# Batch 1's second product as seven block products of two tiles, fourteen of its units in the stretch that makes its input, three half sums of the weights on Pool

## The chip, the cores and the metric

The kernel runs on one core of one Trainium2 chip. The metric is the device time of one execution in microseconds (us); the median of three runs of the kernel before is 203.49 us (203.19 to 203.52). The engines are TensorE (PE), VectorE (DVE), ScalarE (ACT), GpSimd (Pool) and SyncE (SP), each with a queue of its own that it works off in order.

## The reference

For each of 8 batches an attention read between 512 tokens x and 32 state rows (8 heads of 64) gives 512 rows "xread" and 32 rows "sread"; both go through a feed-forward network with weights of 512 x 2048 and 2048 x 512 and a leaky relu between.

```python
scores = scale * x @ state.T          # per batch and head: 512 x 32
a = softmax(scores);   xread = a @ state
scores2 = scale * state @ x.T         # 32 x 512
a2 = softmax(scores2); sread = a2 @ x
x = concat([xread, sread]) as rows of 512 (8 heads x 64): 8 * 544 rows
h = x @ w_in; g = max(0.01 * h, h); out = g @ w_out
```

## The kernel before, in words

**First product, by batch.** xread @ w_in is taken together: M = state @ w_in (`a_m`, evicted by `m_evict`) is small, and `ff1(a, hT, s)` gives block s (of 16) of the hidden layer as M's columns times the softmax `aT` (two matmuls of 512 columns into a PSUM tile of tag ph, which has two buffers), after which ACT's Prelu (L397) writes block s of hT. `ff1_pair` does two blocks into the bank "big", with one Prelu (L407). The 16 steps s = 0 to 15 of a batch are one stretch.

**Second product.** hT @ w_out is done in two ways. `piece(b, hT, i, jq)` (L599) does a quarter of the 16 blocks for one tile i of 128 tokens, with four matmuls of 512 columns. `Batch` does four tiles at once by a seven-product scheme for 2 x 2 block matrices: the blocks are A11, A12, A21, A22 of hT and B11 to B22 of w_out, four sums of each (`Fast.sums` su0 to su3 on DVE, L659; `weights_sum` tw0 to tw3, L636), and products n in the order 1, 2, 6, 5, 7, 3, 4. A unit (n, m) (L670) is one of eight terms of product n: one matmul of 256 columns for each tile row, two with `Batch`, one with `Half`. Two banks of tag py take all seven products in turn: product 1, 6, 7 and 4 one after the other on the first, 2, 5 and 3 on the second. Between them ACT copies the bank out (`save`, L679) and DVE joins it to an earlier copy (`join`, L682).

**Which batch uses what.** Batch 0 uses pieces for all four tiles. Batch 1 uses pieces for tiles 0 and 1 and `Half(h1)` for tiles 2 and 3. Batches 2 to 7 use `Batch`. Of a batch's 56 units, 15 (OWN) are done in its own stretch, the rest in the next one's; `PACE` lists how many units follow each ff1, and `PACE2` does so for batch 2's stretch, where `Half` does its own.

**The softmaxes of the next batch** are worked in the current stretch: `a_scores` (L211), then on DVE `a_shift` (L221, L229, L234), `a_max2` (L283, L285), on ACT `a_exp` (L241) and twice `a_exp2` (L291), on DVE `a_probs` (L246, L250, L253, L258, L259: aT) and `a_probs2` (L297, L299: the reciprocal of the row sums r2). In batch 1's stretch that is a2, and in batch 2's a3.

**Buffers.** The tiles of pool att have two buffers unless they say otherwise; r2, which a_exp2 opens (L290) and a_probs2 reads, has two. A tile that takes over a buffer waits for the last reader of the one before it. The four tw tiles lie in buffers of their own.

**Order.** Nothing is scheduled: the order of each engine's queue is that of the program text. The loop of batch 1's stretch is L1061 to L1083, that of batches 2 to 7 is L1097 to L1229.

Of the kernel before, what the change touches and what calls it, by code (L numbers as in the profile page):

```python
# [9 lines left out]
P = 128  # L10
# [3 lines left out]
DM = 512  # L14
# [16 lines left out]
def kernel(  # L31
# [9 lines left out]
    nc = tc.nc  # L41
# [229 lines left out]
    def a_exp(a):  # L271
        a.e1 = block_exp(a.sh, NB)
# [415 lines left out]
    class Batch:  # L688
        def __init__(self, b, hT):
            saved = {n: (spool, t, 1) for n, t in ((1, "sv1"), (6, "sv6"), (5, "sv1"), (7, "sv7"))}  # L690
            self.b, self.f = b, Fast(hT[:], 2 * P, [(spool, f"su{n}", 1) for n in range(4)], saved)
            self.units = [(n, m) for n in (1, 2, 6, 5, 7, 3, 4) for m in range(NM)]
            own = [(n, m) for n in (1, 2) for m in range(6)] + [(1, 6), (2, 6), (1, 7)]
            assert len(own) == OWN
            self.units = own + [u for u in self.units if u not in own]
            self.bank = {}
            self.yos = {}
# [51 lines left out]
                f.join(self.yo(1)[:, :, :HC], bank, 7)  # L749
                self.out(1)  # L750

    class Half(Batch):


        def __init__(self, hT):
            super().__init__(1, hT)
            self.f.__init__(hT[:, :, 2 * P:], P, self.f.homes, self.f.saved)
            self.units = [(n, m) for n in (1, 2, 6, 5, 7, 3, 4) for m in range(NM)]

        def yo(self, r):  # L760
            if r not in self.yos:
                self.yos[r] = ypool.tile([P, 1, DM], FP32, name="ysb", tag="ysb", bufs=3)
            return self.yos[r]

        def out(self, r, cols=slice(0, DM), i=None, eng=nc.sync):
            eng.dma_start(rows_of(1)[2 + r], self.yo(r)[:, 0, :])

    OWN = 15
    PACE = (1, 4, 4, 4, 3, 4, 4, 3, 4, 4, 4, 4, 3, 4, 3, 3)
    PACE2 = (0,) * 10 + (3, 3, 2, 2, 2, 3)  # L770

    att_of = [Attn() for _ in range(B)]
    a0, a1, a2 = att_of[:3]
# [269 lines left out]
    a_probs(a1)  # L1043
    for i in range(NT):
        piece(0, h0, i, 2)
    for i in (2, 3):
        piece(0, h0, i, 3, copy=None)
    for i in (2, 3):
        y_store(0, i, VEC)
    for h in range(0, H, 2):  # L1050
        cast_x(3, h, h + 2, POO)
    a_a2t(a0)
    weights_sum(2, 4, 8)
    weights_sum(1, 4, 8)
    weights_sum(0)

    h1 = hpool.tile([P, 16, S], BF16, name="hT", tag="hT")
    fill = [(0, h0, 0, 3), (0, h0, 1, 3)] + [(1, h1, i, jq) for jq in range(3) for i in range(2)]  # L1060
    for s in range(16):  # L1061
        if s in (6, 10):
            ff1_pair(a1, h1, s, "big")
        elif s not in (7, 11):
            ff1(a1, h1, s)
        if s % 2:
            pb, hT, i, jq = fill[s // 2]
            piece(pb, hT, i, jq)
        if s == 3:
            a_scores(a2)  # L1070
            m_evict(a2, 0, a_m(a2, 0, "big"), SCA)
            a_shift(a2)
            a_max2(a2)
            a_probs2(a0)
        if s == 7:
            a_exp(a2)
            a_probs(a2)
            a_open(att_of[3], 3)
            a_xt_dma(att_of[3])
        elif s in (9, 11):  # L1080
            a_exp2(a2, s // 2 - 4)
        if s in (5, 9):
            load_state(1, range(s // 2 - 2, s // 2))  # L1083

    a_probs2(a2)
    pm = [a_m(a2, 1, "big"), a_m(a2, 2, "sc")]
    m_evict(a2, 1, pm[0], VEC)
    m_evict(a2, 2, pm[1], SCA)  # L1090
    a_probs2(a1)
    a_a2t(a1)

    before, half = None, Half(h1)
    for b in range(2, B):  # L1097
        hT = hpool.tile([P, 16, S], BF16, name="hT", tag="hT")
        a = att_of[b]
        nxt = att_of[b + 1] if b + 1 < B else None  # L1100
        now = Batch(b, hT)
        std = []
        if b == 2:
            std = [(i, 3) for i in range(2)]
            for n in (0, 1):
                half.f.sums(n)

        def fill(s):
            units((PACE2 if b == 2 else PACE)[s])

        def units(n):
            left = min(n, len(before.units)) if before else 0
            if left:
                before.run(left)
            if n > left:
                now.run(n - left)

        for s in range(16):
            fast = nxt is None and 4 <= s < 12
            if fast:  # L1120
                n = 1 if s in (7, 11) else 2
                k = PACE[s]
                for i in range(n):
                    fl.product()
                    units((i + 1) * k // n - i * k // n)
            elif s == 11:
                fill(s)
            if not fast:
                ff1(a, hT, 4 + s if nxt is None and s < 4 else s)
            if s == 0:  # L1130
                if b + 2 < B:
                    load_x(b + 2, nc.sync)
                a_a2t(a)
                if before:
                    for n in (0, 1):
                        before.f.sums(n, 4, 8)
            elif s == 1:
                if nxt is not None:
                    a_scores(nxt)
                m_evict(a, 3, a_m(a, 3, "big"), SCA)  # L1140
                if b == 2:
                    a_sread_rows([a0])
                elif b % 2:
                    a_sread_rows([att_of[b - 2], att_of[b - 1]])
                if b == 2:
                    half.f.sums(2)
                    a_shift(nxt, 0)
                elif nxt is not None:
                    a_shift(nxt)
                if b + 2 < B:  # L1150
                    open_xb(b + 2)
                    for h in range(0, H, 2):
                        cast_x(b + 2, h, h + 2, POO)
                if before:
                    before.f.sums(2, 4, 8)
            elif s == 3:
                if before:
                    before.f.sums(3)
                if nxt is not None and b > 2:
                    a_max2(nxt)  # L1160
            elif s == 4:
                if b == 2:
                    state_t(1)
                elif b == 4:
                    sread_t(0, 3)
                elif b == 7:
                    sread_t(1, 4)
            elif s == 8:
                if nxt is None:
                    a_sread(a)  # L1170
            elif s == 12:
                for n in range(3):
                    now.f.sums(n, 0, 4)
            if nxt is None:
                if s == 1:
                    fl = FastLast(a, hT)
                    fl.sums()
                elif s in (6, 10):
                    fi.w_sum({6: 1, 10: 3}[s])
                elif s == 13:  # L1180
                    fl.flush()
                    fi.x_sums()
            elif b >= B - 3 and s == 14:
                if b == B - 3:
                    fi = FastIn(None)
                fi.w_sum(2 * (b - (B - 3)))
            if s == (9 if b == 2 else 7) and b + 2 < B:
                a_open(att_of[b + 2], b + 2)
                a_xt_dma(att_of[b + 2])
            if nxt is not None:  # L1190
                if b == 2 and s < 11:
                    if s in (8, 9):
                        a_exp2(nxt, s - 8)
                elif s == 5:
                    a_exp(nxt)
                elif s in (7, 8):
                    a_exp2(nxt, s - 7)
                    if s == 7:
                        a_probs(nxt)
                elif s == 11:  # L1200
                    a_probs2(nxt)
                elif s in (12, 13):
                    SCA(nxt.M[:, s - 12, DM:2 * DM], pm1[:, s - 12, :])
            if std:
                i, jq = std.pop(0)
                piece(1, h1, i, jq)
            elif b == 2 and half.units:
                half.run(7)
                if s == 4:
                    a_shift(nxt, 1)  # L1210
                    half.f.sums(3)
                    weights_sum(3)
                    a_max2(nxt)
                elif s == 6:
                    a_exp(nxt)
                elif s == 8:
                    a_probs(nxt, 0)
            elif s != 11 and not fast:
                fill(s)
            if s == 10 and nxt is not None:  # L1220
                pm0 = a_m(nxt, 0, "big")
                pm1 = a_m(nxt, 1, "sc")
                pm2 = a_m(nxt, 2, "ph")
                for g, copy in enumerate((VEC, SCA)):
                    copy(nxt.M[:, g, 2 * DM:3 * DM], pm2[g][:])
                m_evict(nxt, 0, pm0, SCA)
                if b == 2:
                    a_probs(nxt, 1)
# [91 lines left out]
```

## Time and profile before

| | |
|---|---|
| median of three runs | 203.49 us |
| the profiled execution | 203.07 us, span 201.3 us |
| PE busy | 194.1 us (96%) |
| DVE, ACT, Pool busy | 157.1 (78%), 145.3 (72%), 47.3 us (24%) |
| granted PE clock | 0.998 |
| batch 1's stretch on PE | from 36.5 us |
| batch 2's stretch on PE | 51.7 to 71.9 us |
| a stretch of batches 3 to 7 | about 21 us |

The span is the time from the first to the last instruction; the 1.8 us around it belong to the execution as well. A listed duration holds an end that the next instruction overlaps, so the rate of an engine is read from starts. A line number such as L670 is one of the kernel; helpers have one line for all their uses.

### The profile page before, as it was taken

Reading aid. Unit: us, or ns where it says so; the run is one execution under the profiler, and the core shown is the slowest. Engines: PE = TensorE matmul, PEld = TensorE weight load, DVE = VectorE, ACT = ScalarE, POOL = GpSimd, SP = SyncE. Lnnn points to the kernel's source line nnn. Section 1 sums busy time; section 2 is a strip of 40 time slices with the busy share of each in tenths; the row PEclk is TensorE's granted clock in tenths of the full one; section 3 lists DMA queues with packets and bytes.
Section 4 is the critical chain, followed back from the end, with each engine's and each line's share of the span. In section 5 each row is a group of like instructions: output and inputs, shape, how many; then the busy total and the mean of one; then the engine's idle time right before and its main releaser. Section 6 shows DMA issues by size and latency. Waiting matters only on the chain.

```text
span 201.3 us, 4920 instructions
## 1 busy us (share of the span) xinstructions
PE 194.1 (96%) x2020; PEld 132.2 (66%) x2042; DVE 157.1 (78%) x242; ACT 145.3 (72%) x268; POOL 47.3 (24%) x76
## 2 busy tenths in 40 slices
PE   7899999999999999999999999999999999999993
PEld 2567633444377567766776677676766688799882
DVE  1676689798789889975997599779978977995622
ACT  3478747689869886978697868787878768767710
POOL 8841065040018004200420040200020014104250
PEclk9999999999999999999999999999999999999999
DMA  6999997999692993249433975250027101310035
GB/s 172 225 206 260 248 293 132 205 249 251 101 297 65 223 246 76 44 180 262 88 68 136 283 54 111 104 156 5 0 92 172 29 0 72 139 52 3 0 93 171
DMA packets 40758, 28.01 MB, mean 139 GB/s; under 512 B 25312, under 2 KB 37728, under 8 KB 40736
## 3 DMA queue, kind: packets, MB, share of 16 engines
q1 hardware_dynamic: 35536, 20.88, 43.0%
q0 software_dynamic: 4912, 6.55, 15.9%
q8 instruction: 16, 0.26, 0.5%
q10 hardware_dynamic: 288, 0.26, 0.5%
q14 instruction: 6, 0.05, 0.1%
HBM read 17.30 MB, written 8.91 MB: 130 GB/s over the span
## 4 chain that ended last, share of the span: by engine, by line
PE 80%; DMA 15%; POOL 2%; issue 1%; DVE 0%; POOLq 0%
PE yq L670 40%; PE ph L392 20%; DMA w_out_bf<-in_moe_w_out_dram 10%; DMA w_in_bf<-in_moe_w_in_dram 5%; PE py L599 4%; PE pf L466 3%; PE yu L670 3%; PE pm L371 3%; PE pl L555 2%; PE psn L337 1%; PE sc L211 1%; PE pyw L599 1%; PE phw L403 1%; POOL w_in_bf L123 1%; PE yz L670 0%
## 5 line engine op out<-in xcount | busy, mean ns | idle before, releaser
L397 ACT ACTIVATE hT<-ph 128x512 bf16<-128x512 f32 x100 | 58.9, 605 | 17.3 <-PE ph L392 13.1
L392 PE MATMUL ph<-aT,M 128*128 128x512 bf16 x183 | 54.9, 379 | 0.3
L670 PEld LDWEIGHTS <-su 128*128 128x128 bf16 x448 | 42.9, 98 | 13.8 <-DVE su L659 0.8
L670 PEld LDWEIGHTS <-hT 128*128 128x128 bf16 x312 | 30.1, 98 | 13.5 <-issue 2.0
L670 PE MATMUL yq<-tw_xf,su 128*128 128x256 bf16 x208 | 29.6, 273 | 0.3
L670 PE MATMUL yq<-w_out_bf,hT 128*128 128x256 bf16 x208 | 29.2, 273 | 0.1
L111 POOL CAST xb<-xl 128x512 bf16<-128x512 f32 (+1 forms) x24 | 14.3, 638 | 59.1 <-DMA xl<-in_x_dram 45.1
L392 PEld LDWEIGHTS <-M 128*128 128x128 bf16 x200 | 19.4, 98 | 7.2 <-issue 1.0
L659 DVE TENSOR_TENSOR su<-hT 128x1024 bf16<-128x1024 bf16 x26 | 17.9, 688 | 7.1 <-ACT hT L397 7.1
L740 POOL TENSOR_TENSOR yo<-sv,sv 128x512 f32<-128x512 f32 x6 | 7.8, 1302 | 41.0 <-ACT sv L679 25.4
L679 ACT COPY sv<-yq 128x512 f32<-128x512 f32 (+1 forms) x28 | 15.4, 554 | 2.1 <-PE yq L670 1.4
L599 PEld LDWEIGHTS <-hT 128*128 128x128 bf16 x96 | 9.0, 98 | 10.9 <-issue 1.3
L599 PE MATMUL py<-w_out_bf,hT 128*128 128x512 bf16 x60 | 15.4, 379 | 0.3 <-issue 0.2
L670 PE MATMUL yq<-tw_x,su 128*128 128x256 bf16 x104 | 14.6, 273 | 0.1
L670 PE MATMUL yq<-w_out_bf,su 128*128 128x256 bf16 x104 | 14.5, 273 | 0.2
L385 ACT CAST M<-pm 128x1024 bf16<-128x1024 f32 x13 | 13.2, 1014 | 0.9 <-PE pm L371 0.8
L670 PE MATMUL yq<-tw_x,hT 128*128 128x256 bf16 x96 | 13.6, 273 | 0.0
L682 DVE TENSOR_TENSOR yo<-yq,sv 128x512 f32<-128x512 f32 x17 | 11.6, 684 | 1.5 <-PE yq L670 1.5
L291 ACT ACTIVATE e<-sc,mcols 128x512 bf16<-128x512 f32 x16 | 11.0, 693 | 0.2 <-DVE mcols L285 0.2
L283 DVE TENSOR_REDUCE mcol<-sc 128x2 f32<-128x1024 f32 x8 | 9.7, 1216 | 0.0
L659 DVE TENSOR_TENSOR su<-su,hT 128x1024 bf16<-128x1024 bf16 x13 | 9.0, 692 | 0.4
L221 DVE TRANSPOSE_TENSOR_REDUCE mrow<-sc 128x32 f32<-128x1024 f32 x7 | 8.7, 1243 | 0.6 <-PE sc L211 0.5
(173 smaller groups left out, 299.0 us busy)
## 6 DMA issues: line engine op xcount, KB each, us to landing
xl<-in_x_dram SPq DMA_DIRECT2D x5, 1024.0 KB, 6.9
out_dram<-yo SPq DMA_DIRECT2D x10, 512.0 KB, 2.8
w_in_bf<-in_moe_w_in_dram POOLq DMA_DIRECT2D x4, 512.0 KB, 9.1
w_out_bf<-in_moe_w_out_dram POOLq DMA_DIRECT2D x4, 512.0 KB, 17.7
out_dram<-ysb SPq DMA_DIRECT2D x8, 256.0 KB, 5.7
xf<-in_x_dram SPq DMA_DIRECT2D x2, 512.0 KB, 5.1
x<-in_x_dram POOLq DMA_DIRECT2D x2, 512.0 KB, 14.1
xl<-in_x_dram POOLq DMA_DIRECT2D x1, 1024.0 KB, 20.4
```

Source lines behind the costliest of these rows:

```text
L111: copy(xs[b][:, :, h0:h1].rearrange("p t h d -> p h t d"), xl[b][:, h0:h1].rearrange("p h (t d) -> p h t d", t=NT),)
L221: nc.vector.tensor_reduce(out=m1[:], in_=flat.rearrange("p (c j) -> p c j", j=NS), axis=AX.X, op=ALU.max, apply_transpose=True,)
L283: nc.vector.tensor_reduce(out=m2[:], in_=a.sc[:], axis=AX.X, op=ALU.max, negate=True)
L291: nc.scalar.activation(out=a.e2[:, g], in_=a.sc[:, g, :], func=AF.Exp, bias=a.m2s[:, g:g + 1], scale=SCALE, accum_out=a.r2[:, g:g + 1],)
L385: copy(a.M[:, :, cols], pm[:])
L392: nc.tensor.matmul(ph[:], lhsT=a.M[:, g, P * j:P * (j + 1)], rhs=a.aT[:, g, :], start=(g == 0), stop=(g == 1),)
L397: nc.scalar.activation(out=hT[:, j, :], in_=ph[:], func=AF.Prelu, alpha=0.01)
L599: nc.tensor.matmul(y.py, lhsT=hT[:, j, P * i:P * (i + 1)], rhs=w_out_bf[:, j, :], start=(j == 0), stop=(j == 15),)
L659: (eng or nc.vector).tensor_tensor(out=S[n][:, ms], in0=u[:, ms], in1=v[:, ms], op=op)
L670: nc.tensor.matmul(bank[:, i, :], lhsT=lhs[:, m, P * i:P * (i + 1)], rhs=rhs[:, m, :], start=(first and m == 0 and (i == 0 or of is not No ...
L679: copy(t[:], bank)
L682: nc.vector.tensor_tensor(out=dst, in0=bank, in1=self.sv[n][:], op=ALU.add)
```

## The change

Batch 1 becomes a `Batch` like the others and `Half` goes. Its own units, fourteen and in an order by column pairs, are spread over the steps 7 to 15 of its own stretch (`early`), where its pieces were, and the other 42 lie in batch 2's stretch under a new PACE2. The last pieces of batch 0 move: tile 2 ends before the stretch, tile 3 in its step 1, tiles 0 and 1 in steps 3 and 5. `a_probs2(a0)` moves from step 3 to step 7, behind `a_probs(a2)`. Of the sums of w_out, tw0 (two halves) and the second half of tw3 go to Pool, and the first half of tw3 stays on DVE in batch 2's stretch. There the scores of a3 and what follows them go from step 1 to step 2, and a3's exponentials to steps 7 to 9, `a_exp2` now ahead of `a_exp`.

```diff
@@ class Batch, __init__
             own = [(n, m) for n in (1, 2) for m in range(6)] + [(1, 6), (2, 6), (1, 7)]
-            assert len(own) == OWN
+            if b == 1:
+                own = [(n, 2 * c + m) for c in range(3) for n in (1, 2) for m in range(2)] + [(1, 6), (2, 6)]
+            self.ahead = len(own)
...
-    class Half(Batch):
...
-    PACE2 = (0,) * 10 + (3, 3, 2, 2, 2, 3)
+    PACE2 = (2, 1, 1, 3, 4, 4, 4, 4, 4, 4, 4, 4, 4, 5, 5, 4)
@@ ahead of batch 1's stretch
-    for i in (2, 3):
-        piece(0, h0, i, 3, copy=None)
-    for i in (2, 3):
-        y_store(0, i, VEC)
+    piece(0, h0, 2, 3, copy=None)
+    weights_sum(2, 4, 8)
+    weights_sum(1, 4, 8)
+    weights_sum(3, 4, 8, nc.gpsimd)
+    weights_sum(0, 0, 4, nc.gpsimd)
     for h in range(0, H, 2):
         cast_x(3, h, h + 2, POO)
+    weights_sum(0, 4, 8, nc.gpsimd)
     a_a2t(a0)
-    weights_sum(2, 4, 8)
-    weights_sum(1, 4, 8)
-    weights_sum(0)
@@ batch 1's stretch
-    fill = [(0, h0, 0, 3), (0, h0, 1, 3)] + [(1, h1, i, jq) for jq in range(3) for i in range(2)]
+    before = Batch(1, h1)
+    early = {7: 3, 8: 1, 9: 2, 10: 1, 11: 2, 12: 1, 13: 2, 14: 1, 15: 1}
     for s in range(16):
...
-        if s % 2:
-            pb, hT, i, jq = fill[s // 2]
-            piece(pb, hT, i, jq)
+        if s == 1:
+            piece(0, h0, 3, 3, copy=None)
+            for i in (2, 3):
+                y_store(0, i, VEC)
+        elif s in (3, 5):
+            piece(0, h0, s // 2 - 1, 3)
+        else:
+            before.run(early.get(s, 0))
         if s == 3:
             a_scores(a2)
             m_evict(a2, 0, a_m(a2, 0, "big"), SCA)
             a_shift(a2)
             a_max2(a2)
-            a_probs2(a0)
         if s == 7:
             a_exp(a2)
             a_probs(a2)
+            a_probs2(a0)
             a_open(att_of[3], 3)
             a_xt_dma(att_of[3])
         elif s in (9, 11):
             a_exp2(a2, s // 2 - 4)
...
-    a_probs2(a2)
     pm = [a_m(a2, 1, "big"), a_m(a2, 2, "sc")]
+    for n in (0, 1):
+        before.f.sums(n, 0, 4)
     m_evict(a2, 1, pm[0], VEC)
     m_evict(a2, 2, pm[1], SCA)
-    a_probs2(a1)
+    for a in (a2, a1):
+        a_probs2(a)
     a_a2t(a1)
-    before, half = None, Half(h1)
@@ batch 2's stretch
-            elif s == 1:
+            elif s == (2 if b == 2 else 1):
                 if nxt is not None:
                     a_scores(nxt)
...
                 if b == 2:
-                    half.f.sums(2)
                     a_shift(nxt, 0)
+                    before.f.sums(2)
+                    a_max2(nxt)
+                    before.f.sums(3)
+                    a_shift(nxt, 1)
+                    weights_sum(3, 0, 4)
...
                 if b == 2 and s < 11:
-                    if s in (8, 9):
-                        a_exp2(nxt, s - 8)
+                    if s in (7, 8):
+                        a_exp2(nxt, s - 7)
+                    elif s == 9:
+                        a_exp(nxt)
+                        a_probs(nxt, 0)
...
-            if std:
-                i, jq = std.pop(0)
-                piece(1, h1, i, jq)
-            elif b == 2 and half.units:
-                half.run(7)
-                if s == 4:
-                    a_shift(nxt, 1)
-                    half.f.sums(3)
-                    weights_sum(3)
-                    a_max2(nxt)
-                elif s == 6:
-                    a_exp(nxt)
-                elif s == 8:
-                    a_probs(nxt, 0)
-            elif s != 11 and not fast:
+            if s != 11 and not fast:
                 fill(s)
```

More of the change, by code (lines that the diff above doesn't have):

```diff
@@ L750, in done @@
                 self.out(1)
-    class Half(Batch):
[L755 to L766, printed above, removed]
     OWN = 15
     PACE = (1, 4, 4, 4, 3, 4, 4, 3, 4, 4, 4, 4, 3, 4, 3, 3)
-    PACE2 = (0,) * 10 + (3, 3, 2, 2, 2, 3)
+    PACE2 = (2, 1, 1, 3, 4, 4, 4, 4, 4, 4, 4, 4, 4, 5, 5, 4)
     att_of = [Attn() for _ in range(B)]
@@ L1045 @@
         piece(0, h0, i, 2)
-    for i in (2, 3):
-        piece(0, h0, i, 3, copy=None)
-    for i in (2, 3):
-        y_store(0, i, VEC)
+    piece(0, h0, 2, 3, copy=None)
[3 more added lines that the diff above has]
+    weights_sum(0, 0, 4, nc.gpsimd)
     for h in range(0, H, 2):
         cast_x(3, h, h + 2, POO)
+    weights_sum(0, 4, 8, nc.gpsimd)
     a_a2t(a0)
-    weights_sum(2, 4, 8)
-    weights_sum(1, 4, 8)
-    weights_sum(0)
     h1 = hpool.tile([P, 16, S], BF16, name="hT", tag="hT")
-    fill = [(0, h0, 0, 3), (0, h0, 1, 3)] + [(1, h1, i, jq) for jq in range(3) for i in range(2)]
+    before = Batch(1, h1)
+    early = {7: 3, 8: 1, 9: 2, 10: 1, 11: 2, 12: 1, 13: 2, 14: 1, 15: 1}
+    assert sum(early.values()) == before.ahead
     for s in range(16):
@@ L1101 @@
         now = Batch(b, hT)
[L1102 to L1106, printed above, removed]
         def fill(s):
@@ L1111, in units @@
         def units(n):
-            left = min(n, len(before.units)) if before else 0
+            left = min(n, len(before.units))
             if left:
@@ L1133 @@
                 a_a2t(a)
-                if before:
-                    for n in (0, 1):
-                        before.f.sums(n, 4, 8)
-            elif s == 1:
+                for n in (0, 1):
+                    before.f.sums(n, 4, 8)
+            elif s == (2 if b == 2 else 1):
                 if nxt is not None:
@@ L1153 @@
                         cast_x(b + 2, h, h + 2, POO)
-                if before:
+                if b > 2:
                     before.f.sums(2, 4, 8)
[L1156 to L1159, printed above, removed]
+            elif s == 3 and b > 2:
+                before.f.sums(3)
+                if nxt is not None:
                     a_max2(nxt)
```

## The prediction

> **What bounds the kernel now.** I read the share table of the page first, then the waits of TensorE (PE), then the timelines of PE, ScalarE (ACT) and VectorE (DVE) from 34 to 90 us, where the change lies. The page gives PE busy for 96% of the span; the waits, asked from 30 to 100 us, show that nothing holds it up there:
>
> ```profile
> PE 194.1 (96%) x2020; PEld 132.2 (66%) x2042; DVE 157.1 (78%) x242; ACT 145.3 (72%) x268; POOL 47.3 (24%) x76
> ```
>
> ```profile
> PE py L599 <- issue: 0.2, 1, 0.2
> PE pyw L599 <- DMA w_out_bf<-in_moe_w_out_dram: 0.2, 1, 0.2
> ```
>
> So PE is a full queue: each us of work taken from it is a us gained, and each us that it is made to wait is a us lost, since no later gap can take it up. Its rates come from where a row starts and the next one starts (a listed duration contains an overlapped end):
>
> ```profile
> 75.53 1.04 PE L670 MATMUL yq<-tw_xf,su 128*128 128x256 bf16 x8
> 76.41 0.59 PE L392 MATMUL ph<-aT,M 128*128 128x512 bf16 x2
> 76.84 1.04 PE L670 MATMUL yq<-tw_xf,su 128*128 128x256 bf16 x8
> ```
>
> Eight matmuls of 256 columns take 0.88 us, 0.109 each, and two of 512 take 0.43, 0.216 each. A unit of two tiles is 0.22 us, an ff1 0.43.
>
> The third view is what feeds PE around 45 us, in the stretch where h1 is made. ACT:
>
> ```profile
> 43.43 1.02 ACT L407 ACTIVATE hT<-phw 128x1024 bf16<-128x1024 f32 x1 [0.60 <-PE phw L403]
> 44.44 1.06 ACT L241 ACTIVATE e<-sh 128x1024 bf16<-128x1024 f32 x1
> 45.40 1.06 ACT L397 ACTIVATE hT<-ph 128x512 bf16<-128x512 f32 x2
> 46.35 0.69 ACT L291 ACTIVATE e<-sc,mcols 128x512 bf16<-128x512 f32 x1
> ...
> 47.02 1.03 ACT L407 ACTIVATE hT<-phw 128x1024 bf16<-128x1024 f32 x1
> ```
>
> and DVE:
>
> ```profile
> 45.51 0.17 DVE L285 TENSOR_SCALAR mcols<-mcol 128x2 f32<-128x2 f32 x1
> 45.58 0.16 DVE L297 TENSOR_SCALAR r<-r 128x2 f32<-128x2 f32 x1
> 45.78 0.17 DVE L299 RECIPROCAL qall<-r 128x2 f32<-128x2 f32 x1
> 45.86 1.22 DVE L246 TRANSPOSE_TENSOR_REDUCE r<-e 128x32 f32<-128x1024 bf16 x1
> ...
> 49.00 0.69 DVE L259 TENSOR_TENSOR aT<-e,qb 128x1024 bf16<-128x1024 bf16 x1
> 49.61 0.16 DVE L297 TENSOR_SCALAR r<-r 128x2 f32<-128x2 f32 x1
> 49.81 0.17 DVE L299 RECIPROCAL qall<-r 128x2 f32<-128x2 f32 x1
> ```
>
> The reader is to see the pair at 45.58 and 45.78: a_probs2(a0), done before the long row a_probs(a2) (L246 to L259) begins, and before ACT's first a_exp2(a2) at 46.35. From the start of L246 to the end of the pair that closes the row are 4.12 us (45.86 to 49.98).
>
> **The work on PE.** Out go 32 matmuls of 512 columns (tiles 0 and 1 of batch 1): 32 x 0.216 = 6.91 us. In come 56 of 256 columns (seven products, eight terms, now two tiles): 56 x 0.109 = 6.10. That is -0.81 us, all on the path.
>
> **What is hidden.** ACT's copies for batch 1 go from two of 0.59 and four of 0.37 to four of 0.59, DVE's joins from three of 0.42 to three of 0.68; neither is a bound over the stretch. On Pool three half sums of 2.12 each (the row of L636 on Pool) fall into its idle 33.9 to 43.3 and 45.6 to 59.6; they end by 47.8, and PE's first use of them is behind 60. On SyncE's queue a_a2t(a0) now goes ahead of four output stores instead of two; the xT of a2, issued at 33.95, lands after 4.3, at 38.3, and is wanted at 39.2; the xT of a3 keeps its place near 45.6, lands 5.3 later and is wanted at 56. Nothing for these; with the cover gone, some tenths each. ff1(a1, 0) now stands right behind the third quarter-pieces, at 35.66, just when DVE's aT of a1 ends (34.97 + 0.69): 0.06 us of signal, as in the row where an ACT copy ended at 8.895 and PE went on at 8.95.
>
> **The wait that the change adds.** r2, the row sums of a_exp2, has two buffers in the att pool: a0 and a1 hold them, and a2 gets a0's back once a_probs2(a0) has read it. The change moves a_probs2(a0) from step 3, ahead of a_probs(a2), to step 7, behind it. In the built program ACT's first a_exp2(a2) now waits for that reciprocal. Queued behind it on ACT is the relu of the pair 10/11, and PE's unit (1,5), in step 12, reads h1 block 10. With PE dense from 35.72: units begin at 42.4, step 12's ff1 ends at 46.33 and (1,5) is due at 46.55. ACT has relu 9 done by 45.6. DVE: scores of a2 at 39.3, L221 from 39.76, then 4.96 to L285 (40.55 to 45.51 before), L246 from 44.79, L299 done 4.12 later, at 48.91. ACT goes on at 48.95: a_exp2 0.67, relu 1.03, signal 0.06: 50.71. **PE waits 4.16 us** and then 0.05 for a ph bank.
>
> **The second wait.** Batch 1's product 1 now ends in batch 2's step 0, and unit (6,0) needs its bank two ff1 later, where ACT has M's copy, a relu and the copy of the product to do. From the end of the two M products (53.80) PE gets there in 1.30 us (an ff1, two units, an ff1: 55.10). ACT starts at 53.95: 0.91 + 0.49 + 0.59 + 0.06, so 56.00. +0.90.
>
> **The third: DVE's order in batch 2's stretch.** With a_scores(a3) moved to step 2, DVE starts the row of a3 when the psn product ends, at 57.8, and then has in its queue: L346 0.20, L221 and L229 2.56, a sum of 2048 1.13, max2 1.33, a second such sum 1.13, shift 1.14: 65.4. ACT's a_exp2(a3) waits in the built program for that shift, and stands ahead of relu 8, the other a_exp2, a copy, relu 9, the exponential and relu 10 (4.3 us: 69.75). PE is at the second bank of its ph product at 68.87, and waits for relu 10 until 69.81: +0.94. The exponential ends at 69.26; DVE then does L246 to L253 and a join (2.35) and at 71.65 the M copy that ff1(12) needs, done 72.34; PE is there at 71.40: +1.00. Then DVE has L258, L259, two small ones, three sums and the join of product 4 until 77.01, and batch 2's unit (2,0) needs that join's bank; PE is there at 75.65: +1.42.
>
> One thing in it has no row in place: whether Pool's casts of x 4 (from 59.5) slow the DVE sum at 60.6. A two-input DVE row of this width took 1.22 alone and 1.62 beside those casts:
>
> ```profile
> 39.32 1.22 DVE L636 TENSOR_TENSOR tw_xf<-w_out_bf 128x2048 bf16<-128x2048 bf16 x1
> 60.68 1.62 DVE L636 TENSOR_TENSOR tw_x<-tw_xf,w_out_bf 128x2048 bf16<-128x2048 bf16 x1
> ```
>
> I take the second, as it stands in the same place: +0.40, with 0 and 0.8 (both sums) as its ends. The Trainium skill, "SBUF — State Buffer", section "Who interferes with whom", says that a DVE instruction with two SBUF inputs contends with a GpSimd instruction that reads SBUF, the later one blocking for the whole of the other; by that rule a Pool half sum can also hold L259 up, by 2.1 us at most. The trace agrees as to the casts (1.62 against 1.22). I keep the rows.
>
> **Sum.** -0.81 + 0.06 + 4.16 + 0.05 + 0.90 + 0.94 + 1.00 + 1.42 + 0.40 = +8.1. From the end of that stretch on (PE 71.85 before, near 80 after) orders are the same, and DVE's relation to PE too: DVE's first sum there begins 0.2 behind PE's mark before, and at it after. The profiled execution took 203.07 (span 201.3 and 1.8 around it), so 211.2 on its account, 211.6 on the median's 203.49. The late terms are differences of long sums, and a row that is shorter in its new place shrinks them: I say 211.0.
>
> **Rivals.** (a) Only the first waits cost: DVE catches up, and the third group is not there. Then -0.81 + 0.06 + 4.21 + 0.90 = +4.4, 207.5 from 203.07. For it: DVE is idle near 67 us in my reckoning. Against: each of its terms is an order in a queue. (b) The idle PE comes back slow. The first row of the trace shows a slow PE:
>
> ```profile
> 1.20 3.17 PE L137 MATMUL pspin<-idle 128*128 128x512 bf16 x7 [1.20 <-DVE warm L74]
> ```
>
> 3.1 us to the next row for seven of 512, 0.44 each, and about half rate to nearly 6 us, against 0.216 later, though the granted clock reads 1.00. Should 4.16 us of idleness bring that back for 3.4 to 4.8 us, half of it is lost, 1.7 to 2.4: about 213.1. No gap of before is over 0.5 us, so no row says from where it decides. The Trainium skill, "TensorE: Matmul & The Clock Gate", section "What's actually happening", has the clock halve after an idle window of some 3.4 us that runs free. By that a gap of 4.16 holds a whole window about one time in five. (c) The other sign: the wait has cover. If a_exp2(a2) did not hold the pair's relu (it decides at a stall under 0.8 us in all), PE would keep dense: 203.07 - 0.81 + 0.1, so 202.4 to 202.8. For it speaks that ACT is idle 28% of the span; against, that the wait is in ACT's own queue, and that PE has two units and an ff1 to do until it reads the block.
>
> **Chances.** The forecast, 209 to 212.3, 0.63; (a), 206.5 to 209, 0.13; (b), 212.3 to 213.6, 0.17; (c) 0.05; between, 0.02. The range from 207.2 to 213.2 leaves out (c), the lower part of (a), and the upper end of (b): two in ten. About 0.2%, 0.4 us, can be told from no change: faster 0.05, same 0.02, slower 0.93.
>
> **What would show it.** In the changed profile: PE idle for about 4 us before a unit (L670) near 46.5, released by ACT's relu L407; ACT idle 3.3 us before a_exp2 (L291), released by DVE's L299; then PE waits near 55 (ACT's L679), 69 (ACT's L397), 71.4 (DVE's M copy) and 75.6 (DVE's L682). PE at 0.43 per 512 columns behind the gap would be (b); no gap near 46.5 would make the forecast wrong at its root.

## The result and the profile after

The changed kernel takes 214.7 us (median of four runs, 213.57 to 215.3) against 203.34 for the kernel before beside it: a ratio of 1.0553, with an interval of 1.0504 to 1.0603. The profiled execution took 215.3 us, with a span of 213.5. It is slower, as predicted, and by more than the range allowed for (213.2).

The share line of the page and its row of the granted clock:

```profile
PE 198.4 (93%) x2066; PEld 135.3 (63%) x2066; DVE 159.8 (75%) x243; ACT 146.2 (68%) x266; POOL 54.5 (26%) x79
...
PEclk9999999997599999999999999999999999999999
```

PE's share falls from 96% to 93%, and the clock row, all nines before, has a 7 and a 5 in the tenth and eleventh slice, about 48 to 59 us. The waits of PE, over the whole span (us in total, times, the longest):

```profile
PE yq L670 <- ACT hT L407: 5.3, 1, 5.3
PE yq L670 <- DVE yo L682: 1.2, 1, 1.2
...
PE yq L670 <- DVE su L659: 0.8, 1, 0.8
PE pm L371 <- ACT hT L397: 0.8, 1, 0.8
PE ph L392 <- DVE M L1204: 0.7, 1, 0.7
...
PE ph L392 <- DVE aT L259: 0.3, 1, 0.3
```

All six are waits that the kernel before does not have. The first is the gap in batch 1's stretch; here is PE's timeline around it (start, duration, and in brackets the idle time before the row):

```profile
46.63 0.59 PE L392 MATMUL ph<-aT,M 128*128 128x512 bf16 x2
52.52 0.61 PE L670 MATMUL yq<-w_out_bf,hT 128*128 128x256 bf16 x2 [5.29 <-ACT hT L407]
52.92 1.06 PE L392 MATMUL ph<-aT,M 128*128 128x512 bf16 x2
53.77 1.06 PE L670 MATMUL yq<-w_out_bf,hT 128*128 128x256 bf16 x4
```

The gap ends at unit (1,5), as forecast. Behind it two matmuls of 512 take 0.85 us by the starts (52.92 to 53.77), where they took 0.43 before. The table of windows gives the granted clock there (behind the stretch and its length, PE's busy time; the last three columns are the clock, the DMA share and GB/s):

```profile
50.00:52.00 2.00, 0.00 (x0) 0.00 (x0) 1.93 (x5) 1.23 (x3) 0.00 (x0) 0.80 0.38 83
52.00:54.00 2.00, 1.48 (x6) 0.73 (x7) 0.05 (x1) 1.62 (x4) 0.00 (x0) 0.50 0.79 158
...
58.00:60.00 2.00, 1.67 (x16) 0.70 (x8) 1.91 (x6) 1.65 (x3) 0.00 (x0) 0.99 0.29 66
```

In finer windows the clock falls to 0.50 at 51.2, while PE is still idle, and comes back to 1.00 at 58.0. And what came ahead of the gap, on ACT, DVE and Pool:

```profile
50.77 0.69 ACT L291 ACTIVATE e<-sc,mcols 128x512 bf16<-128x512 f32 x1 [4.60 <-DVE qall L299]
```

```profile
45.21 1.49 DVE L285 TENSOR_SCALAR mcols<-mcol 128x2 f32<-128x2 f32 x1
46.62 1.23 DVE L246 TRANSPOSE_TENSOR_REDUCE r<-e 128x32 f32<-128x1024 bf16 x1
...
50.57 0.17 DVE L299 RECIPROCAL qall<-r 128x2 f32<-128x2 f32 x1
```

```profile
44.55 2.13 POOL L636 TENSOR_TENSOR tw_xf<-w_out_bf 128x1024 bf16<-128x1024 bf16 x1
```

ACT stands still before the first a_exp2(a2), for the reciprocal of a_probs2(a0), as forecast. But DVE's L285, a row of two elements for each partition that took 0.17 before, takes 1.49: it ends at 46.70, when Pool's third half sum ends (46.68).

The scores of a3, batch 3's, are a mark in both traces behind all of this: L211 stands at 73.03 before and at 85.02 after, 11.99 later. By the starts of the rows this is made up so:

| term | predicted | in the trace after |
|---|---|---|
| work taken from PE | -0.81 | -0.81 (by count) |
| later start, less the wait for w_out that is gone | 0 | +0.12 |
| ff1(a1, 0) waits for aT | +0.06 | +0.44 |
| gap before unit (1,5), and the ph bank | +4.21 | +5.46 |
| clock at 0.50 behind it | 0, or 1.7 to 2.4 as rival (b) | +2.6 |
| second wait, unit (6,0) | +0.90 | +0.98 |
| third group: the M product, ff1(12), unit (2,0) | +0.94, +1.00, +1.42 | +0.95, +0.88, +1.42 |
| Pool's casts beside the sum of 2048 | +0.40 | +0.07 |
| sum | +8.1 | +12.0 |

The 2.6 is the stretch from (1,5) to the end of the next M products, 5.68 us here (52.52 to 58.20) and 3.10 in the first experiment below, where the same rows run at full clock. The 0.07 lies in the third group already and is not added to the right-hand sum.

### The profile page after: what moved, and what is told of

Its sections match the earlier page's. It is cut to its first block, busy times and chain, and to the rows that moved or that the text cites. A ratio compares the mean times of both kernels' runs of the same rounds, so it can differ in the third digit from the quotient of the medians.

```text
span 213.5 us, 4989 instructions
## 1 busy us (share of the span) xinstructions
PE 198.4 (93%) x2066; PEld 135.3 (63%) x2066; DVE 159.8 (75%) x243; ACT 146.2 (68%) x266; POOL 54.5 (26%) x79
## 4 chain that ended last, share of the span: by engine, by line
PE 75%; DVE 19%; ACT 3%; issue 1%; DVEq 0%
PE yq L670 35%; PE ph L392 17%; PE pf L466 3%; PE pm L371 3%; PE yu L670 3%; PE pspin L137 2%; DVE su L659 2%; PE ph L942 2%; DVE mrowb L229 2%; DVE mrow L221 2%; DVE qb L258 2%; DVE sh L234 2%; DVE r L246 2%; DVE mcol L283 2%; PE pl L555 2%; PE sc L211 1%
## 5 line engine op out<-in xcount | busy, mean ns | idle before, releaser
L397 ACT ACTIVATE hT<-ph 128x512 bf16<-128x512 f32 x100 | 59.1, 603 | 23.6 <-PE ph L392 23.0
L392 PE MATMUL ph<-aT,M 128*128 128x512 bf16 x200 | 59.8, 387 | 1.0 <-DVE M L1204 0.7
L670 PEld LDWEIGHTS <-su 128*128 128x128 bf16 x480 | 45.9, 98 | 16.2 <-DVE su L659 2.1
L670 PE MATMUL yq<-w_out_bf,hT 128*128 128x256 bf16 x224 | 32.8, 279 | 6.5 <-ACT hT L407 5.3
L670 PE MATMUL yq<-tw_xf,su 128*128 128x256 bf16 x224 | 31.9, 273 | 0.8 <-DVE su L659 0.8
L659 DVE TENSOR_TENSOR su<-hT 128x1024 bf16<-128x1024 bf16 (+1 forms) x27 | 19.1, 709 | 9.1 <-ACT hT L397 9.1
L742 POOL TENSOR_TENSOR yo<-sv,sv 128x512 f32<-128x512 f32 x7 | 9.1, 1297 | 44.0 <-ACT sv L679 26.6
L679 ACT COPY sv<-yq 128x512 f32<-128x512 f32 x28 | 16.3, 585 | 2.4 <-PE yq L670 1.7
L670 PE MATMUL yq<-tw_x,su 128*128 128x256 bf16 x112 | 15.7, 273 | 0.0
L682 DVE TENSOR_TENSOR yo<-yq,sv 128x512 f32<-128x512 f32 x20 | 13.6, 682 | 1.5 <-PE yq L670 1.5
L246 DVE TRANSPOSE_TENSOR_REDUCE r<-e 128x32 f32<-128x1024 bf16 x7 | 8.7, 1238 | 3.3 <-ACT e L241 3.3
L659 DVE TENSOR_TENSOR su<-su,hT 128x1024 bf16<-128x1024 bf16 x14 | 9.7, 692 | 0.5
```

The costliest lines, as they stand in the source:

```text
L246: nc.vector.tensor_reduce(out=r1[:], in_=e1[:].rearrange("p (c j) -> p c j", j=NS), axis=AX.X, op=ALU.add, apply_transpose=True,)
L392: nc.tensor.matmul(ph[:], lhsT=a.M[:, g, P * j:P * (j + 1)], rhs=a.aT[:, g, :], start=(g == 0), stop=(g == 1),)
L397: nc.scalar.activation(out=hT[:, j, :], in_=ph[:], func=AF.Prelu, alpha=0.01)
L659: (eng or nc.vector).tensor_tensor(out=S[n][:, ms], in0=u[:, ms], in1=v[:, ms], op=op)
L670: nc.tensor.matmul(bank[:, i, :], lhsT=lhs[:, m, P * i:P * (i + 1)], rhs=rhs[:, m, :], start=(first and m == 0 and (i == 0 or of is not No ...
L679: copy(t[:], bank)
```

## The experiments

The theory after the result: the waits simply add up on a full PE. The root is the order of a_probs2(a0); the Pool half sum makes that gap longer; idleness halves the clock; the second wait and the third group are orders of their own. The rival: batch 1's pairs of tiles bring DVE and ACT more than the stretch holds, so that any mended wait comes back somewhere else.

### a_probs2(a0) back in step 3

```diff
             a_max2(a2)
+            a_probs2(a0)
         if s == 7:
             a_exp(a2)
             a_probs(a2)
-            a_probs2(a0)
```

> The changed kernel with a_probs2(a0) put back into step 3, ahead of a_probs(a2); the rest as changed. Theory (the r2 wait makes a PE gap of 5.4 us, and the gap halves PE's clock for 5.6 us, 2.6 us lost): ACT's a_exp2(a2) waits only for DVE's L285, which a Pool half sum still holds up to about 46.7 us, so PE's gap before (1,5) shrinks to about 1.5 us, the clock stays at 1.00, and the time is 214.7 - 4.0 - 2.6 = 208 us. Rival 1 (the Pool half sum is the chief cause, the place of a_probs2 is not): the gap stays over 4 us and the time at 213 or more. Rival 2 (most is lost in batch 2's stretch): the time falls by 4 us at most.

Measured: 208.51 us (207.66 to 209.34), ratio 1.0259 (1.0222 to 1.0296), clock 0.999. The gap before (1,5) is 0.58, no slow stretch follows it, and the other waits stand (0.8, 0.8, 0.9, 1.3). One edit, which moves two tiny rows of DVE (0.16 and 0.17), gives back 6.2 of the 11.4 us by the medians. Pool's half sum, which runs from 45.76 to 47.88 here, holds another row, which takes 0.18 in the kernel before:

```profile
46.70 1.22 DVE L250 TENSOR_SCALAR r<-r 128x32 f32<-128x32 f32 x1
```

It ends at 47.92, again as the half sum ends.

### The third half sum ahead of x[3]'s casts

```diff
+    weights_sum(0, 4, 8, nc.gpsimd)
     for h in range(0, H, 2):
         cast_x(3, h, h + 2, POO)
-    weights_sum(0, 4, 8, nc.gpsimd)
```

> The changed kernel with its third half sum on Pool (second half of tw0) ahead of the casts of x 3 instead of behind them. Theory: it is done by 44 us, DVE's L285 takes 0.17 us again instead of 1.49, and the gap of PE shrinks by 1.3 us to about 4.1. If a gap of 4.1 us still halves the clock: 213.4 us; if it does not: 210.7 us. Rival 1 (the Pool half sum is the chief cause): the gap falls below 1 us and the time to about 207. Rival 2 (DVE's long L285 has another reason): L285 stays at 1.5 us and the time at 214.7.

Measured: 213.47 us (212.49 to 214.02), ratio 1.0498 (1.0467 to 1.0528), clock 0.984.

```profile
PE yq L670 <- ACT hT L407: 4.2, 1, 4.2
```

```profile
44.91 0.42 DVE L285 TENSOR_SCALAR mcols<-mcol 128x2 f32<-128x2 f32 x1
```

Without the half sum beside it, L285 is 1.07 shorter (0.42; Pool's casts run beside it here, where 0.17 was the row's time before), and the gap is 4.21, near the forecast's 4.16. So 1.1 of the gap's 5.3 us is the half sum's. By the times alone the two kernels are not told apart (212.49 to 214.02 here, 213.57 to 215.3 for the changed one); the rows show it. The gap of 4.2 halves the clock all the same, from 48.9, when PE has been idle for 2.0 us, until 55.8:

```profile
48.60:48.90 0.30, 0.00 (x0) 0.00 (x0) 0.30 (x1) 0.00 (x0) 0.00 (x0) 1.00 1.28 289
...
49.10:49.40 0.30, 0.00 (x0) 0.00 (x0) 0.27 (x3) 0.01 (x1) 0.00 (x0) 0.50 1.27 284
```

### Spins in the gap

```diff
     for s in range(16):
+        if s == 12:
+            spin(24, "ph")
```

Twenty-four matmuls on a tile of no meaning keep PE busy while it would wait.

> The changed kernel with 24 matmuls on the zero tile (5.2 us of PE work, results unused) in PE's queue ahead of ff1 12, so that PE is busy while it would wait for h1's block 10. Theory (the clock halves because PE is idle): the granted clock stays at 1.00 all through, unit (1,5) starts about when it did, and the time falls by the 2.6 us that the half clock costs, to about 212.1 us. Rival (the low clock has another reason than the idle time): the clock falls to 0.5 all the same, and the time stays at 214.7 or rises.

Measured: 212.08 us (211.86 to 212.25), ratio 1.0436 (1.0419 to 1.0454), clock 0.999 and 1.00 in every window from 46 to 62. ACT still waits 4.50 for L299:

```profile
49.97 0.69 ACT L291 ACTIVATE e<-sc,mcols 128x512 bf16<-128x512 f32 x1 [4.50 <-DVE qall L299]
```

So the gap's cause is unchanged; what is gone, 2.6 us of the median, is the half clock alone. It is due to PE's idleness, and it is a cost beside the wait. (Here it is L250 that the half sum holds, for 1.41.)

### The kernel before with a_probs2(a0) late

The kernel before, with this one call moved from step 3 to step 7, behind a_probs(a2); nothing else of the change.

> The kernel before, with one thing of the change alone: a_probs2(a0) in step 7, behind a_probs(a2). No Pool half sum runs there. Theory: ACT's a_exp2(a2) waits for DVE's L299 until about 49.9 us, the relu of blocks 10 and 11 ends at 51.6, and PE, whose piece (1, 0, 2) is due at 48.4, waits about 3.2 us: 206.5 us if the clock stays at 1.00, up to 2 more if it halves. Rival 1 (the place of a_probs2 does not matter): 203.4 us.

Measured: 207.95 us (206.45 to 208.31), ratio 1.0217 (1.0179 to 1.0256), clock 0.992. So the order alone costs 4.8 us, without Pool's sums and without the new products.

```profile
PE py L599 <- ACT hT L407: 2.5, 1, 2.5
...
PE ph L392 <- ACT hT L397: 0.5, 1, 0.5
```

```profile
52.00:54.00 2.00, 1.45 (x6) 0.49 (x5) 0.34 (x2) 1.69 (x5) 0.00 (x0) 0.77 0.80 154
54.00:56.00 2.00, 2.00 (x13) 0.56 (x19) 0.00 (x0) 0.60 (x1) 0.00 (x0) 0.50 0.84 232
56.00:58.00 2.00, 1.95 (x22) 0.62 (x8) 1.47 (x4) 1.18 (x2) 0.00 (x0) 0.87 1.54 329
```

The gap is shorter, since here the pair's relu is wanted later. Yet 2.5 us of idleness, a little work and another 0.5 were enough for the clock to fall: in finer windows it is 0.50 from 53.1 to 56.5, which is 1.7 us lost. 2.48, 0.55 and 1.7 make 4.7 of the 4.8. It is not so each time: one of the four executions kept a mean clock of 1.0 and took 206.45, 3.3 above the kernel before and so little more than the two waits; the other three, at 0.991 and 0.992, took 207.83 to 208.31.

### Both first moves

a_probs2(a0) back in step 3 and the third half sum ahead of the casts.

> After, with a_probs2(a0) back in step 3 and the third half sum on Pool ahead of x[3]'s casts. If the waits simply add: the 5.3 gap and the half clock are gone (208.5 in the run with a_probs2(a0) back), and the remaining gap of 0.58 ahead of unit (1,5), which stood behind the row L246 to L259 that Pool's half sum stretched from 3.14 to 4.18, shrinks by up to 0.6: 207.9 to 208.2. The second wait (about 0.9) and the third group (about 3.2) stay. The rival, that the work of batch 1's pairs is too much for VectorE and ScalarE in its stretch, expects the 0.58 to stay or to move: 208.5.

Measured: 208.29 us (208.25 to 208.36), ratio 1.0229 (1.0215 to 1.0243). No gain beyond the first move alone, and the gap before (1,5) is 0.95, not less: my reason for the 0.58 was wrong. It did not stand behind L246 to L259. In both kernels ACT has the first a_exp2(a2) (0.69) ahead of the pair's relu. And with the half sum earlier, the casts move under DVE's two tiny rows instead:

```profile
45.14 0.42 DVE L285 TENSOR_SCALAR mcols<-mcol 128x2 f32<-128x2 f32 x1
45.48 0.65 DVE L297 TENSOR_SCALAR r<-r 128x2 f32<-128x2 f32 x1
```

L297 takes 0.16 with Pool idle. It ends at 46.13, and Pool's casts (43.81, for 2.29) at 46.10; ACT waits 0.26 for what follows it.

### The second wait

```diff
-    PACE2 = (2, 1, 1, 3, 4, 4, 4, 4, 4, 4, 4, 4, 4, 5, 5, 4)
+    PACE2 = (0, 2, 2, 3, 4, 4, 4, 4, 4, 4, 4, 4, 4, 5, 5, 4)
```

> The changed kernel with a_probs2(a0) back in step 3, the third half sum ahead of x[3]'s casts, and one more edit: the product units of the paced stretch run 0, 2, 2, 3 instead of 2, 1, 1, 3 in its first steps, so that unit (6,0) comes after the other work of the first step and its bank has been copied out. If the second wait is this order alone: 0.9 less than without that edit, about 207.1. The rival (too much work for VectorE and ScalarE) expects the wait to return at the next unit whose bank the same copies hold: no gain.

Measured: 208.29 us (207.79 to 208.88), ratio 1.023 (1.0211 to 1.0248). The wait of 0.80 before (6,0) is gone and the time is the same. Part of it comes back at once, as an ff1 that waits for ACT's relu (0.23); from the scores of a2 to the ff1 and units at 55.8 PE is 0.58 faster (15.49 against 16.07). The rest goes ahead of the third group:

```profile
64.71 0.59 PE L392 MATMUL ph<-aT,M 128*128 128x512 bf16 x2 [0.27 <-ACT hT L397]
```

By the starts this row comes 0.43 later behind its units than its twin without the edit (64.71 - 63.41 against 64.27 - 63.40), and the three waits of the third group follow unchanged (0.8, 0.9, 1.3). They hang on the chain of a3's softmax on DVE and ACT, and PE that comes there sooner waits sooner. Neither reason that I gave is the whole one: the wait is the order's, and its gain is lost to the next wait as long as that stands.

### The third group

```diff
                     before.f.sums(2)
-                    a_max2(nxt)
-                    before.f.sums(3)
                     a_shift(nxt, 1)
+                    before.f.sums(3)
+                    a_max2(nxt)
...
-            elif s == 12:
+            elif s == (13 if b == 2 else 12):
                 for n in range(3):
                     now.f.sums(n, 0, 4)
...
-                    if s in (7, 8):
-                        a_exp2(nxt, s - 7)
-                    elif s == 9:
+                    if s == 7:
                         a_exp(nxt)
                         a_probs(nxt, 0)
+                    elif s in (8, 9):
+                        a_exp2(nxt, s - 8)
```

> As the kernel with the pace of 0, 2, 2, 3, and the third group's order mended too: the joins of two-tile blocks stand ahead of the sums on VectorE, the exponentials of the next batch's last two tiles behind those of the first two, and batch 2's first sums one step later. If the three waits of the third group (0.8, 0.7 and 1.2 in the changed kernel) are of that order alone, they go: about 3.2 less, 203.9. The rival, too much work for VectorE and ScalarE in the stretch, expects them to come back at other units: 206 or more.

Measured: 204.66 us (204.41 to 206.52), ratio 1.0064 (1.0038 to 1.009): 3.6 us less, and none of the three waits is left in the list. Here it was the order, with no lack of time on DVE or ACT. (The joins that "stand ahead of the sums" are, in the diff, the second half of the shift ahead of the second sum, and batch 2's first sums, which go a step later and so behind a join.)

### Batch 0's last pieces as before

Tiles 2 and 3 both ahead of the stretch, so that ff1(a1, 0) comes behind them.

> As the kernel with the third group's order mended, with batch 0's last pieces of tiles 2 and 3 both ahead of the stretch too, as the kernel before has them, so that the first ff1 of the stretch does not wait for aT (0.44). If all waits of the changed kernel are then gone, what is left of the change is the matrix work that it takes away, 0.81: 202.3 to 203.5, at or below the kernel before. The rival expects 205 or more.

Measured: 204.38 us (204.19 to 204.9), ratio 1.0041 (1.0028 to 1.0055): 0.3 less, which the intervals do not tell from none. The wait for aT (0.44) is gone, but with the piece of step 1 gone too, the first ff1s stand in a row, and the third one waits for ACT's relu: 0.42 by the starts, the 0.25 at 38.0 below. Still above the kernel before, with the 0.59 before (1,5) and two waits for a relu (0.25 at 38.0 and 0.23 at 52.7) in the list.

### Four tries at what is left

In the first, a_exp2(a2) goes to steps 11 and 12, behind the pair's relu.

> The kernel with all mends so far (204.4), with a_exp2(a2) at steps 11 and 12 instead of 9 and 11: in that kernel's trace unit (1,5) still waits 0.59 for ScalarE's L407, which stands behind the first L291 (0.69 and the read of 0.19). Theory, the waits add up: L407 starts 0.7 earlier, the 0.59 goes, 203.8. Rival, the work is too much for ScalarE: a wait of about the same size comes at a later ff1 whose bank ScalarE has not emptied, 204.4.

Measured: 204.13 us, ratio 1.0039 (1.0024 to 1.0055). The 0.59 is gone, and an ff1 waits 0.34 for its bank instead; no gain that can be told. In the second the pace is 1, 1, 2, 3 as well.

> As the kernel with a_exp2(a2) at steps 11 and 12, with a pace of 1, 1, 2, 3 in place of 0, 2, 2, 3: unit (6,0) stays behind the psn product, and each of the first ff1s has a unit behind it. In the kernel with all mends but these two, two ff1s waited 0.23 and 0.25 for ScalarE's relu. Theory: these go, 0.4 to 0.5 less, 203.3. Rival, too much work for ScalarE: no change, 203.8.

Measured: 204.12 us, ratio 1.0034 (1.0022 to 1.0046). No change, as the rival had it. In the third the half sum is on DVE as well, in its place ahead of the casts.

> As the kernel with the pace of 1, 1, 2, 3, with the half sum weights_sum(0,4,8) on VectorE in place of Pool, the way the kernel before has it. VectorE is not late in that place once the waits are mended, so its 0.69 costs nothing there, and what Pool's casts hold of L285 and L297 ends 2.1 earlier. Theory: no change within 0.3, since nothing on TensorE waits for these rows any more. Rival: that row is still on the path, and the time falls by up to 0.6.

Measured: 203.88 us, ratio 1.0028 (1.0019 to 1.0036). Within the 0.3 that the theory gave; the gain, if there is one, is not told apart from none. In the fourth a_exp2(a2) goes to steps 12 and 14 as well.

> As the kernel with the half sum on VectorE, with a_exp2(a2) at steps 12 and 14 instead of 11 and 12, so that two relu rows lie between ScalarE's two pairs of exponentials. In that kernel ff1s still wait 0.50 and 0.39 for ScalarE's relu by the starts of TensorE's rows. Theory, orders alone: the 0.50 goes, ratio to the kernel before 1.000 to 1.001. Rival, the stretch is full (in that kernel's trace ScalarE is busy 4.59 of the 5 us from 48 on, VectorE 4.86, against 3.95 and 3.26 in the kernel before): the wait moves to the next ff1, the ratio stays near 1.003.

Measured: 203.88 us (203.33 to 204.06) beside 203.46 for the kernel before, ratio 1.0018 (1.0006 to 1.0029). This is the best version of the change by its ratio, and it does not beat the kernel before. The windows of the end of batch 1's stretch show a part of why, first the kernel before and then this one (busy us of PE, PEld, DVE, ACT and Pool, with the number of rows in brackets):

```profile
48.00:53.00 5.00, 4.95 (x37) 2.00 (x37) 3.26 (x7) 3.95 (x9) 0.00 (x0) 1.00 1.06 147
```

```profile
48.00:53.00 5.00, 4.64 (x53) 2.09 (x51) 4.86 (x10) 4.96 (x12) 0.00 (x0) 1.00 0.57 124
```

DVE and ACT are now full in these 5 us, 4.86 and 4.96, and PE is the one with gaps. In this place the rival's forecast fits: a wait that is mended comes back as another one, small. But this place is not all of it. From the first ff1 of batch 1's stretch to the scores of a3 the kernel before takes 36.51 us (36.52 to 73.03) and this one 37.20 (36.46 to 73.66), with 0.81 less of matrix work in it. By the starts of its rows, PE here loses 0.93 in small waits from 46.5 to 52.2, 0.42 ahead of the third ff1 at 37.74, and 0.39 in the M product at 64.36 (24 matmuls in 1.16, where they took 0.77 before). The last two make as much as the 0.81, and no run mended them.

## Why the prediction was wrong in size

**Right: the sign, and each wait's place and, but for one, its releaser.** The gap at 46.6 with ACT waiting for L299, (6,0), relu L397 before the M product, DVE's M copy before ff1(12), the join before (2,0): all are in the trace. The one is (6,0): ACT's copy L679 was forecast and DVE's sum L659 is named, but the copy ends at 60.33 and the first of the sums at 60.37, and in the first experiment it is the copy. The places are right, and the last four terms are within 0.12 us of what was worked out. Moving one call back took out the first, and a new order on DVE and ACT took out the third group (3.6 us, with the 0.5 that the mended second wait had left there, against 3.36 forecast). Rival (a), which left that group out, is refuted; rival (c), that the first wait has cover, too.

**Wrong: "Nothing for these", of the three half sums on Pool.** I looked for idle time on Pool and for PE's first use, and for contention only at L259. The third half sum held a tiny row in the very chain that made the gap: 1.32 us at L285 here, 1.04 and 1.23 at L250 in two experiments, each row ending within 0.04 us of the half sum. With the half sum elsewhere the gap is 4.21, against 4.16 worked out. The profile before had the sign of it: L285 took 0.17 at 45.51, but 0.44 in batch 2's stretch, where it ends with a cast on Pool (63.92 and 63.90):

```profile
63.29 0.61 POOL L181 CAST stb<-stf 128x512 bf16<-128x512 f32 x1
63.48 0.44 DVE L285 TENSOR_SCALAR mcols<-mcol 128x2 f32<-128x2 f32 x1
```

The Trainium skill, "SBUF — State Buffer", section "Who interferes with whom", of which I used the sentence on two inputs, goes on to say that `tensor_scalar` is among the operations that can take the port pair which VectorE shares with GpSimd, and that the later one then blocks fully. The runs agree with that at L285, L250 and L297; of the DVE rows beside the third half sum only L285 and L250, both TENSOR_SCALAR, were long.

**Wrong: rival (b) at 0.17.** It came true, on top of the forecast: +2.6, at the gap that was certain in my own reckoning. The step that failed is "a gap of 4.16 holds a whole window about one time in five". The clock does not need a window that is wholly idle:

| kernel | PE idle | clock at 0.50 | length |
|---|---|---|---|
| the changed one | 47.1 to 52.5 | 51.2 to 58.0 | 6.8 |
| half sum first | 46.9 to 51.1 | 48.9 to 55.8 | 6.8 |
| before, a_probs2(a0) late | 49.0 to 51.5, 52.1 to 52.7 | 53.1 to 56.5 | 3.4 |
| both moves | 0.95 before (1,5), 1.26 before (2,0) | never | |

The slow stretch lasts 3.4 us or twice that. If the 3.4 us before each fall are taken as one window, they hold 3.4, 2.0 and 2.4 us of idle time; in these traces the largest single gap without a fall is the 1.26 us before (2,0) with both moves. The lengths agree with the window of some 3.4 us that runs free, which the Trainium skill gives in "TensorE: Matmul & The Clock Gate", section "What's actually happening". Its wording that an idle window is needed does not agree as I read it: 2.0 us of 3.4 were enough. By that a gap of 4.2 throttles nearly always, and rival (b) was the likeliest case, not one in six. The other executions bear it out: of the eight of the changed kernel and of the one with the half sum first, seven show a mean clock of 0.984 and one 0.992. With the waits of 2.5 and 0.5 us three of four fell. From where between 1.26 and 2.0 us it decides, and what kept the fourth at 1.0, no run shows.

**Wrong by less.** Pool's casts beside the sum of 2048 cost 0.07 and not 0.40: they began at 62.31, for the psn product, and the two sums at 64.93 and 67.47 took 1.29 and 1.22. And ff1(a1, 0) waited 0.44 for aT where 0.06 was worked out.

**Not settled by a term of the sum: "neither is a bound over the stretch".** True of the whole stretch, not of its last 5 us, where the last experiment finds both DVE and ACT full. In the changed kernel this was hidden behind the larger waits. That the fullness keeps the change from gaining is argued from the windows and from four tries that moved the waits about; no run took work off DVE or ACT there. It is not the only candidate: of the small waits that are left, 0.81 lie elsewhere, at 37.74 and 64.36, and whether another order mends them was not tried.

The sum with the two failed steps mended, the half sum from the second experiment and the clock from the first: 8.1 + 1.1 + 2.6 = 11.8, and 203.07 + 11.8 = 214.9, against 215.3 in the profiled execution.

## What to carry to other kernels

When a call is moved past another on an engine's queue, look for who takes over the buffer that it reads: two rows of 0.17 us, moved 4 us later, cost 4.8 us alone. On a PE-bound kernel price a stall of over 2 us at its length and the slow clock behind it (1.7 to 2.6 us here), and fill it with matmuls of no meaning if it cannot be avoided. Work that is moved to an idle Pool is not free while DVE has short TENSOR_SCALAR rows on the path: lay it beside stretches where they wait for nothing, and see afterwards which DVE row ends when Pool's does.

## What was not expected of the hardware

A row of two elements for each partition (L285, 0.17 us) can last 1.49 us beside a Pool sum, and the TRANSPOSE_TENSOR_REDUCE of 1024 right behind it, or beside the same sum in another run, kept its 1.23. And the granted clock falls in the middle of an idle stretch (51.2) or a little after one (53.1), and then holds for 3.4 or 6.8 us, most of it with PE busy again (3.4, and 4.6 to 5.5).
